# The split of wo moved from GpSimd between the stages to ScalarE and VectorE inside the last tile of the first stage

## The chip, the cores and the metric

The kernel runs on one core of a Trainium2 chip. The metric is the time of one execution on the device in microseconds, as the median of several runs; less is better.

## The reference

Two different blocks alternate, on the same x of 2048 rows and 640 columns, all in float32. In short:

```python
def A(x, wqkv, wo):                      # linear attention, 32 heads of 20
    q, k, v = split(x @ wqkv)            # each (head, row, 20)
    phi = lambda t: where(t > 0, t + 1, exp(t)) + 1e-6
    kv = einsum("hsd,hse->hde", phi(k), v)
    z = phi(k).sum(rows)
    o = (phi(q) @ kv) / (phi(q) . z + 1e-6)
    return merge_heads(o) @ wo

def B(x, w1, b1, w2, b2):                # 640 -> 1728 -> 640
    return relu(x @ w1 + b1) ** 2 @ w2 + b2

x = x + A(layernorm(x)); x = x + B(layernorm(x))
x = x + A(layernorm(x)); x = x + B(layernorm(x))   # the same weights again
```

## The kernel before

A pass over A and B is one layer; there are two, with the same code. Each float32 operand of a matmul is kept as a high part, which ScalarE rounds with a copy (`AF.Copy` to fp32r), and a low part, which is the rest and is made by a subtraction, as a rule on VectorE. A product is then three matmuls: high with low, low with high, high with high. `split(hi, lo, src)` does both parts; line 147 is its copy and line 148 its subtraction.

The order of the work on each engine is the order in which the code issues it, written out by hand. Nothing is reordered, so an instruction that waits holds up everything behind it on its engine.

**First stage** (loop at line 746): 16 tiles of 128 rows. For tile t, TensorE computes k and, for most tiles, q (`part`, line 508 through `mm3`, line 418). For the tiles listed in `LATE`, 14 and 15 among them, q is computed after the loop (`late_q`). phi is an exp on ScalarE (line 521) and two operations on VectorE (lines 528 and 529). `k_post` (line 724) splits phi(k) into `kh` and adds it into `acc` on GpSimd (line 731); `acc` is the sum of phi(k) from which z comes. kv is not formed from v: with xh the split normalised x, the stage sums G = xhᵀ·phi(k), in five row blocks of 128 (`g_part`, PSUM banks 3 to 7) for the first 512 columns of phi(k), and the last 128 columns transposed as GT (`gt_part`, one call for two tiles and half of the columns of x, added on VectorE at line 559).

During tiles 13 to 15, `load_vo` loads the v columns of wqkv, and wo in six chunks of 120 rows (the last has 40), into tiles called `uraw`.

**Between the stages** (lines 875 to 1176), in order of issue: two late q products; `ah`, the split of acc, and its column sums with a matrix of ones (line 913), copied to `zbc`; `b_den(0)`, which begins the denominators of tile 0; the last `g_part` of the five blocks, each with a ScalarE copy out of PSUM (line 926); the last two `gt_part`; the rest of `b_blocks(0)`; six `wo_high` copies on ScalarE (line 942, into tiles called `uo`) and six `wo_low` subtractions on GpSimd (line 946); five turns of GT on TensorE (line 387) and their copy Gs; kv for six blocks of heads (line 987), each masked on VectorE (line 992), copied and subtracted into `kvbd` (lines 993 and 997); then M = kv·wo for the six blocks (line 1011), three pairs of PSUM banks in turn. M goes through DRAM and comes back as `Mr`, while TensorE does further late q products; then the output products with M begin (line 439).

The masks of kv use banks 3, 4, 5, 6, 7, 2 in turn, and M the pairs (4,5), (2,3), (6,7): an M product waits for the masks that read its banks.

Tiles named x (xh, kh, ah, uo, pT, kvbd, Mr) share a ring of eight places; phi(k) of a tile, two of the uo and Gs share a ring of three.

**Second stage**: the block B in groups of 512 rows (lines 1229 and 1289), with A's output products for the next group inside it.

Of the kernel before, what the change touches and what calls it, by code (L numbers as in the profile page):

```python
# [8 lines left out]
F32 = mybir.dt.float32  # L9
R32 = mybir.dt.float32r  # L10
AF = mybir.ActivationFunctionType
ALU = mybir.AluOpType

P = 128
S, D, F = 2048, 640, 1728
H, DH = 32, 20
NT = S // P
# [13 lines left out]
NH = -(-D // HR)  # L31
# [53 lines left out]
def head_rows(c):  # L85
    return min(HR, D - HR * c)
# [3 lines left out]
def kernel(  # L90
# [11 lines left out]
    nc = tc.nc  # L102
# [13 lines left out]
    def bank(i, n=1):  # L116
        return PS[:, 512 * i : 512 * (i + n)]
# [23 lines left out]
    def ftile(name):  # L141
        return tmp.tile([P, D], F32, tag="f", name=name, bufs=F_BUFS)


    def split(hi, lo, src):

        nc.scalar.activation(hi, src, AF.Copy)
        nc.vector.tensor_tensor(out=lo, in0=src, in1=hi.bitcast(F32), op=ALU.subtract)  # L148
# [242 lines left out]
    def blocks_T(src):  # L391
        y = ftile("y")
        nc.vector.transpose(out=y, in_=src)  # L393
        return [y]

    def blocks_move(yz, js, vector=False):
        if len(yz) == 1:
            yz.append(ftile("z"))
        yv, zv = (a.rearrange("p (c j q) -> p c j q", c=DC, q=B32) for a in yz)
        for j in js:  # L400
            for i in range(P // B32):
                d, v = zv[j * B32 : (j + 1) * B32, :, i, :], yv[i * B32 : (i + 1) * B32, :, j, :]
                if vector:
                    nc.vector.tensor_copy(d, v)
                else:
                    nc.scalar.activation(d, v, AF.Copy)  # L406
# [7 lines left out]
    def mm3(ps, lh, ll, rh, rl, first, last):  # L414

        seq = [(lh, rl), (ll, rh), (lh, rh)]
        for i, (a, b) in enumerate(seq):
            nc.tensor.matmul(ps, a, b, start=first and i == 0, stop=last and i == 2)  # L418
# [54 lines left out]
    for layer in range(N_LAYERS):  # L473
        src = [rows(t, xf) for t in range(NT)] if layer == 0 else x2
        last_layer = layer == N_LAYERS - 1
        if layer == 0:
# [8 lines left out]
        ap = sg.enter_context(  # L485
            tc.tile_pool(name=f"a_{layer}", bufs=1, side="left", reuse_waits="tile")
        )
# [7 lines left out]
        acc = ap.tile([P, D], F32, name="acc", tag="acc", bufs=1)  # L495
# [4 lines left out]
        def xbank():  # L500
            xbanks.append(xbanks.pop(0))
            return bank(xbanks[-1])

        def part(t, a, b, ps=None):

            ps = (xbank() if ps is None else ps)[:, : b - a]
            for c in range(DC):
                mm3(
                    ps, xT[t][:, 0, c, :], xT[t][:, 1, c, :],
                    kq[c][:, 0, a:b], kq[c][:, 1, a:b], c == 0, c == DC - 1,  # L510
                )
            return ps
# [23 lines left out]
        def xtile(name, dtype=R32):  # L536
            return xp.tile([P, 2, D], dtype, tag="x", name=name, bufs=8)
# [12 lines left out]
        def gt_part(p, j, ps):  # L550

            ps, rs = ps[:, :HD], slice(j * HD, (j + 1) * HD)
            for t in (2 * p, 2 * p + 1):
                a, b = kh[t][:, :, DM:], xh[t][:, :, rs]
                mm3(ps, a[:, 0], a[:, 1], b[:, 0], b[:, 1], t % 2 == 0, t % 2 == 1)
            if p == 0:
                nc.vector.tensor_copy(GT_[:, rs], ps)
            else:
                nc.vector.tensor_tensor(out=GT_[:, rs], in0=ps, in1=GT_[:, rs], op=ALU.add)

        if layer == 0:
# [18 lines left out]
            for ps, a, b in runs:  # L580
                v = xt[0][:, a * P : b * P]
# [10 lines left out]
            for ps, a, b in runs:  # L592
                d = T4[0][:, 0, :, a * P : b * P]
                nc.vector.tensor_tensor(
                    out=d[:, 1], in0=ps[:, : (b - a) * P], in1=d[:, 0].bitcast(F32), op=ALU.subtract
# [16 lines left out]
            out=mask, in_=mask, compare_op=ALU.is_ge, fill=0.0, base=0,  # L612
# [3 lines left out]
            out=mask, in_=mask, compare_op=ALU.is_ge, fill=0.0, base=DH - 1,  # L616
# [3 lines left out]
        vo = {}  # L620
# [68 lines left out]
        def b_blocks(t):  # L689
            b_step(t, 3)  # L690
# [33 lines left out]
        def k_post(t, r, between=()):  # L724

            kh[t] = u = xtile("kh")
            nc.scalar.activation(u[:, 0], r, AF.Copy)
            if t == 0:
                nc.gpsimd.tensor_copy(acc, r)
            else:  # L730
                nc.gpsimd.tensor_tensor(out=acc, in0=acc, in1=r, op=ALU.add)  # L731
            for f in between:
                f()
            nc.vector.tensor_tensor(out=u[:, 1], in0=r, in1=u[:, 0].bitcast(F32), op=ALU.subtract)  # L734

        moved = {}

        def move(t, n=P // B32, vector=False):

            if t in yza:  # L740
                blocks_move(yza[t], range(moved.get(t, 0), n), vector)
                moved[t] = n

        late = LATE[layer]
        q_end = None
        for t in range(NT):
# [15 lines left out]
            if first:  # L762
# [35 lines left out]
                fq.rest()  # L798
                xh[t] = split_new(xt[t], "xh")
                k_post(t, fk.r)  # L800
                nc.sync.dma_start(pqd[0], fq.r)
                continue
# [12 lines left out]
            ps = ps_first if layer == 0 and t == 1 else part(t, 0, n0, bank(XB[0]))  # L815
            gs(0 if is_late or t == 1 and layer == 0 else 2)
            move(t + 1, vector=t in VMOVE)
            f.exp(0, ps)
            second = layer == 0 and t == 1
# [3 lines left out]
            elif not early and t + 2 < NT:  # L823
                a_apply(t + 2)
                yza[t + 2] = blocks_T(xt[t + 2])
            f.rest()
            gt = t % 2 == 0 and t > 0
            ps = part(t, n0, D if is_late else 1024, bank(XB[1]))
            if t + 1 in yza:
# [30 lines left out]
            else:  # L860
                ps = part(t, 1024, 2 * D, bank(XB[2]))
                gs(1)
            k_post(t, f.r, [lambda: a_stats(t + 3)])
            if gt and not is_late:
                gt_part(t // 2 - 1, 1, bank(XB[1]))
            gs(DC)
            if not is_late:

                def q_end(t=t, f=fq, ps=ps):
                    f.exp(1024 - D, ps)  # L870
                    f.rest()
                    nc.sync.dma_start(pqd[t], f.r)

            move(t + 2, AHEAD)
        if q_end:
            q_end()
# [6 lines left out]
        def late_q(n=1, rest=True):  # L883

            for _ in range(n):
                if not late_parts:
                    return
                t, j = late_parts.pop(0)
                if j == 0:
                    late_phi[t] = Phi(ftile("rl"))  # L890
                late_phi[t].exp(j * HD, part(t, D + j * HD, D + (j + 1) * HD))
                late_todo.append((t, j))
                if rest:
                    late_rest()
# [3 lines left out]
        def late_rest(n=9):  # L898
            for _ in range(min(n, len(late_todo))):
                t, j = late_todo.pop(0)  # L900
                late_phi[t].rest()
                if j == 1:
                    nc.sync.dma_start(pqd[t], late_phi.pop(t).r)

        late_q(1)
        ah = xtile("ah")
        split(ah[:, 0], ah[:, 1], acc)
        late_q(1)
        zbc = tmp.tile([P, R_], F32, tag="z", name="zbc", bufs=1)
        psz = [xbank()[:, :HD] for _ in range(2)]  # L910
# [5 lines left out]
        for j in range(JB):  # L916
            p, k = slice(j * B32, (j + 1) * B32), j % 2
            v = psz[j // 2][p, k * R_ : (k + 1) * R_]
# [5 lines left out]
        for i in range(DC):  # L924
            g_part(NT - 1, i)
            nc.scalar.activation(G[:, i], bank(GB[i]), AF.Copy)
        for j in range(2):
            gt_part(NT // 2 - 1, j, xbank())
        b_blocks(0)

        wo_hi = {}

        def wo_high(i):
            n = head_rows(2 * i + 1)
            if i < 2:
                v = xtile("uo")
                wo_hi[2 * i], wo_hi[2 * i + 1] = v[:, 0], v[:, 1]
            else:
                wo_hi[4], wo_hi[5] = (ap.tile([P, D], F32, tag="r", name="uo", bufs=3).bitcast(R32) for _ in range(2))
            for c in (2 * i, 2 * i + 1):  # L940
                n = head_rows(c)
                nc.scalar.activation(wo_hi[c][:n], vo["o", c][:n].bitcast(F32), AF.Copy)

        def wo_low(c):
            n, v = head_rows(c), vo["o", c]
            nc.gpsimd.tensor_tensor(
                out=v[:n], in0=v[:n].bitcast(F32), in1=wo_hi[c][:n].bitcast(F32), op=ALU.subtract
            )

        for i in range(3):  # L950
            wo_high(i)
        for c in range(NH):
            wo_low(c)

        psT = bank(1, 2)
        transpose5(psT, GT_)
# [768 lines left out]
```

## Time and profile before

| | |
|---|---|
| time, median of 3 runs | 1345.42 us (1345.09 to 1345.6) |
| the profiled execution's own time | 1347.59 us |
| its span, first to last instruction | 1345.8 us |
| mean granted TensorE clock | 0.999 |
| TensorE busy | 1334.4 us (99%) |
| VectorE busy | 903.6 us (67%) |
| ScalarE busy | 708.9 us (53%) |
| GpSimd busy | 144.8 us (11%) |

All durations of single instructions come from the profiled execution. PE is TensorE's matmuls and PEld its weight loads, DVE is VectorE, ACT is ScalarE, POOL is GpSimd, SP is the engine that issues most transfers. In a timeline a line has the start and the length in microseconds, engine, line of the code, operation, output and inputs, and in brackets how long the engine had stood idle and who released it. Instructions of one kind that follow each other are merged into one line with their count, and the length is then that of the whole series.

### The profile page before, as it was taken

What the parts mean: (1) busy time and instruction counts of PE and PEld (TensorE: products, weight loads), DVE (VectorE), ACT (ScalarE), POOL (GpSimd) and SP (SyncE); (2) the same over time, 40 slices, a digit from 0 to 9 for tenths busy, and PEclk for the clock granted to TensorE, in tenths of its full rate; (3) what the DMA queues carried; (4) which work ended last, traced back from release to release, by engine and by line L of the source; (5) the groups of instructions that cost most, each with busy time, mean ns of one, the idle gap of its engine ahead of it and who ended that gap; (6) DMA issues with size and microseconds to landing.
All of it is one profiled execution on the core that took longest, in us unless ns stands there. A gap on an engine that the chain in (4) does not pass through costs nothing.

```text
span 1345.8 us, 18849 instructions
## 1 busy us (share of the span) xinstructions
PE 1334.4 (99%) x6770; PEld 1156.1 (86%) x6770; DVE 903.6 (67%) x1613; ACT 708.9 (53%) x1636; POOL 144.8 (11%) x183
## 2 busy tenths in 40 slices
PE   9999999999999999999999999999999999999998
PEld 7888999988888888888888899898888888888887
DVE  8988879877766756543367678688677567665323
ACT  5888854634545426424547686455435535454131
POOL 2222221100000000000012232400000000000000
PEclk9999999999999999999999999999999999999999
DMA  6788835775557476487521115077447565564644
GB/s 205 254 294 318 274 98 160 241 273 174 194 200 234 134 258 184 158 308 290 203 98 53 46 40 153 24 242 264 153 161 270 162 202 190 213 213 142 250 165 158
DMA packets 100687, 257.53 MB, mean 191 GB/s; under 512 B 12802, under 2 KB 37762, under 8 KB 99922
## 3 DMA queue, kind: packets, MB, share of 16 engines
q1 hardware_dynamic: 99370, 253.68, 55.8%
q10 hardware_dynamic: 1224, 2.65, 0.7%
q8 instruction: 53, 0.87, 0.3%
q14 instruction: 40, 0.33, 0.1%
HBM read 197.60 MB, written 60.13 MB: 191 GB/s over the span
## 4 chain that ended last, share of the span: by engine, by line
PE 96%; DVE 3%; DMA 1%; ACT 0%; SPq 0%; issue 0%; POOL 0%; DVEq 0%; ACTq 0%
PE PS L418 36%; PE PS L1289 28%; PE PS L1229 28%; PE PS L439 3%; PE PS L1011 1%; DMA st<-in_A_wqkv_dram 1%; DVE kvbd L997 0%; DVE pT L148 0%; DVE e L528 0%; DVE r L529 0%; DVE pqt L671 0%; DVE bn L373 0%; PE PS L387 0%; SPq L226 0%; ACT kq L204 0%
## 5 line engine op out<-in xcount | busy, mean ns | idle before, releaser
L1229 PE MATMUL PS<-xTb,u 128*128 128x512 f32 x1400 | 332.8, 390 | 0.0
L406 ACT ACTIVATE z<-y 32x160 f32<-32x160 f32 x880 | 294.0, 334 | 61.0 <-DVE y L393 51.1
L1229 PEld LDWEIGHTS PS<-xTb,u 128*128 128x128 f32 x1400 | 262.3, 188 | 53.7
L418 PE MATMUL PS<-kq,xT 128*128 128x320 f32 (+2 forms) x1575 | 282.3, 334 | 0.0
L1289 PE MATMUL PS<-u,h 128*128 128x512 f32 x1120 | 279.6, 390 | 0.0
L418 PEld LDWEIGHTS PS<-kq,xT 128*128 128x128 f32 x1575 | 250.3, 188 | 25.2 <-DVE xT L148 0.2
L1247 ACT ACTIVATE hr<-PS,b1sb 128x512 f32<-128x512 f32 x104 | 71.5, 687 | 348.9 <-PE PS L1229 347.3
L1289 PEld LDWEIGHTS PS<-u,h 128*128 128x128 f32 x1120 | 208.0, 188 | 39.6
L1251 DVE TENSOR_TENSOR hr<-hr 128x512 f32<-128x512 f32 x104 | 71.3, 685 | 148.7 <-ACT h L1248 148.7
L418 PE MATMUL PS<-kh,xh 128*128 128x512 f32 x480 | 124.1, 392 | 0.9 <-DVE kh L734 0.8
L377 POOL TENSOR_SCALAR rs<-mv 128x1 f32<-128x1 f32 x63 | 28.8, 457 | 823.6 <-DVE mv L375 823.6
L521 ACT ACTIVATE e<-PS 128x320 f32<-128x320 f32 (+4 forms) x128 | 53.3, 435 | 100.4 <-PE PS L418 92.3
L418 PEld LDWEIGHTS PS<-kh,xh 128*128 128x128 f32 x480 | 87.2, 188 | 16.0 <-DVE kh L734 1.2
L528 DVE TENSOR_SCALAR e<-e 128x320 f32<-128x320 f32 (+4 forms) x128 | 42.9, 335 | 64.5 <-ACT e L521 64.2
L1289 PE MATMUL PS<-h,u 128*128 128x512 f32 x280 | 79.1, 391 | 0.0
L1252 DVE TENSOR_TENSOR h<-hr,h 128x512 fp32r<-128x512 f32 x104 | 72.0, 693 | 7.5
L731 POOL TENSOR_TENSOR acc<-acc,r 128x640 f32<-128x640 f32 x30 | 53.9, 1796 | 197.4 <-DVE r L529 197.4
L1248 ACT ACTIVATE h<-hr 128x512 fp32r<-128x512 f32 x104 | 65.8, 633 | 3.7 <-DVE uT L148 0.5
L1289 PEld LDWEIGHTS PS<-h,u 128*128 128x128 f32 x280 | 52.0, 188 | 10.5 <-DVE h L1265 0.4
L1497 DVE TENSOR_TENSOR xr<-PS,xr 128x320 f32<-128x320 f32 x48 | 23.5, 489 | 51.8 <-PE PS L418 50.2
L1229 PE MATMUL PS<-xTb,uw 128*128 128x512 f32 x240 | 57.0, 389 | 0.0
L529 DVE SCALAR_TENSOR_TENSOR r<-PS,e 128x512 f32<-128x512 f32 (+2 forms) x104 | 51.1, 492 | 5.8 <-ACT e L521 2.3
(142 smaller groups left out, 1599.7 us busy)
## 6 DMA issues: line engine op xcount, KB each, us to landing
u<-kept_w SPq DMA_DIRECT2D x184, 640.0 KB, 4.7
x<-x SPq DMA_DIRECT2D x48, 320.0 KB, 4.8
kept_w<-uprep SPq DMA_DIRECT2D x23, 640.0 KB, 5.5
pqt<-pq SPq DMA_DIRECT2D x128, 80.0 KB, 4.5
x<-xr SPq DMA_DIRECT2D x32, 320.0 KB, 2.3
st<-in_B_w_dram SPq DMA_DIRECT2D x22, 320.0 KB, 3.4
pq<-r SPq DMA_DIRECT2D x20, 320.0 KB, 2.4
kept_kq<-kq SPq DMA_DIRECT2D x10, 640.0 KB, 5.6
```

Of the source, the lines that this page charges most:

```text
L406: nc.scalar.activation(d, v, AF.Copy)
L418: nc.tensor.matmul(ps, a, b, start=first and i == 0, stop=last and i == 2)
L521: nc.scalar.activation(self.e[:, a:b], ps, AF.Exp)
L528: nc.vector.tensor_scalar(e, e, 1.0, PHI_EPS, op0=ALU.min, op1=ALU.add)
L529: nc.vector.scalar_tensor_tensor(out=self.r[:, a:b], in0=ps, scalar=0.0, in1=e, op0=ALU.max, op1=ALU.add)
L731: nc.gpsimd.tensor_tensor(out=acc, in0=acc, in1=r, op=ALU.add)
L1229: nc.tensor.matmul(ps, a[:, d, :], bb[:, d, :], start=n == 0, stop=n == len(order) - 1)
L1247: nc.scalar.activation(r, ps, AF.Relu, bias=b1sb[:, c : c + 1])
L1248: nc.scalar.activation(h[:, 0], r, AF.Square)
L1251: nc.vector.tensor_tensor(out=r, in0=r, in1=r, op=ALU.mult)
L1252: nc.vector.tensor_tensor(out=h[:, 1], in0=r, in1=h[:, 0].bitcast(F32), op=ALU.subtract)
L1289: nc.tensor.matmul(ps, l, r, start=first and k == 0, stop=last and k == len(a) - 1)
```

## The change

1. `wo_high` and `wo_low` are defined ahead of the loop over tiles. `wo_low` runs on VectorE.
2. In tile 15, after phi of the first half of k and ahead of the second half's product, the first four chunks of wo are split: two copies, two subtractions, two copies, two subtractions.
3. The last two chunks are split right after `ah`, ahead of the second late q product.
4. The last two `gt_part` are issued after the third of the five last `g_part`, in place of after the fifth.
5. In layer 0, tiles 1 and 2, the addition of phi(k) into `acc` is done by VectorE, behind the subtraction that makes the low part of `kh`, in place of by GpSimd ahead of it.

```diff
@@ k_post
             if t == 0:
                 nc.gpsimd.tensor_copy(acc, r)
-            else:
+            elif not (layer == 0 and t in (1, 2)):
                 nc.gpsimd.tensor_tensor(out=acc, in0=acc, in1=r, op=ALU.add)
             for f in between:
                 f()
             nc.vector.tensor_tensor(out=u[:, 1], in0=r, in1=u[:, 0].bitcast(F32), op=ALU.subtract)
+            if layer == 0 and t in (1, 2):
+                nc.vector.tensor_tensor(out=acc, in0=acc, in1=r, op=ALU.add)
@@ ahead of the loop over tiles: wo_high as before, and
+        def wo_low(c):
+            n, v = head_rows(c), vo["o", c]
+            nc.vector.tensor_tensor(
+                out=v[:n], in0=v[:n].bitcast(F32), in1=wo_hi[c][:n].bitcast(F32), op=ALU.subtract
+            )
@@ in the loop
             f.rest()
+            if t == NT - 1:
+                wo_high(0)
+                wo_low(0)
+                wo_low(1)
+                wo_high(1)
+                wo_low(2)
+                wo_low(3)
             gt = t % 2 == 0 and t > 0
             ps = part(t, n0, D if is_late else 1024, bank(XB[1]))
@@ after the loop
         split(ah[:, 0], ah[:, 1], acc)
+        wo_high(2)
+        wo_low(4)
+        wo_low(5)
         late_q(1)
@@
         for i in range(DC):
             g_part(NT - 1, i)
             nc.scalar.activation(G[:, i], bank(GB[i]), AF.Copy)
-        for j in range(2):
-            gt_part(NT // 2 - 1, j, xbank())
+            if i == 2:
+                for j in range(2):
+                    gt_part(NT // 2 - 1, j, xbank())
         b_blocks(0)
-
-        wo_hi = {}
-
-        def wo_high(i):
...
-        def wo_low(c):
-            n, v = head_rows(c), vo["o", c]
-            nc.gpsimd.tensor_tensor(
-                out=v[:n], in0=v[:n].bitcast(F32), in1=wo_hi[c][:n].bitcast(F32), op=ALU.subtract
-            )
-
-        for i in range(3):
-            wo_high(i)
-        for c in range(NH):
-            wo_low(c)
```

More of the change, by code (lines that the diff above doesn't have):

```diff
@@ L742, in move, with wo_high @@
                 moved[t] = n
+        wo_hi = {}
+        def wo_high(i):
+            n = head_rows(2 * i + 1)
+            if i < 2:
+                v = xtile("uo")
+                wo_hi[2 * i], wo_hi[2 * i + 1] = v[:, 0], v[:, 1]
+            else:
+                wo_hi[4], wo_hi[5] = (ap.tile([P, D], F32, tag="r", name="uo", bufs=3).bitcast(R32) for _ in range(2))
+            for c in (2 * i, 2 * i + 1):
+                n = head_rows(c)
+                nc.scalar.activation(wo_hi[c][:n], vo["o", c][:n].bitcast(F32), AF.Copy)
+        def wo_low(c):
[3 more added lines that the diff above has]
+            )
         late = LATE[layer]
@@ L926 @@
             nc.scalar.activation(G[:, i], bank(GB[i]), AF.Copy)
-        for j in range(2):
-            gt_part(NT // 2 - 1, j, xbank())
+            if i == 2:
+                for j in range(2):
+                    gt_part(NT // 2 - 1, j, xbank())
         b_blocks(0)
-        wo_hi = {}
-        def wo_high(i):
[L934 to L942, printed above, removed]
-        def wo_low(c):
-            n, v = head_rows(c), vo["o", c]
-            nc.gpsimd.tensor_tensor(
-                out=v[:n], in0=v[:n].bitcast(F32), in1=wo_hi[c][:n].bitcast(F32), op=ALU.subtract
-            )
-        for i in range(3):
-            wo_high(i)
-        for c in range(NH):
-            wo_low(c)
         psT = bank(1, 2)
```

## The prediction

> **What bounds the kernel now.** I read the page first: its first part (busy time), then the chain that ended last.
>
> ```profile
> span 1345.8 us, 18849 instructions
> PE 1334.4 (99%) x6770; PEld 1156.1 (86%) x6770; DVE 903.6 (67%) x1613; ACT 708.9 (53%) x1636; POOL 144.8 (11%) x183
> ...
> PE 96%; DVE 3%; DMA 1%; ACT 0%; SPq 0%; issue 0%; POOL 0%; DVEq 0%; ACTq 0%
> ```
>
> TensorE holds 96% of the chain and the 11.4 us in which it is idle are all that an edit of the other engines can win, beside time in which its clock is lowered. The change adds and removes no matmul. So the next view is the list of TensorE's own waits, cut to the lines that the change can reach:
>
> ```profile
> PE PS L1011 <- DVE kvr L992: 3.7, 4, 1.4
> ...
> PE PS L418 <- DVE kh L734: 0.8, 1, 0.8
> PE PS L387 <- DVE GT L559: 0.7, 2, 0.4
> ```
>
> These 5.2 us are two waits for VectorE in each layer between the stages (the products M = kv·wo at L1011, the turns of GT at L387) and one in the first tiles (L418). Whoever made VectorE late is seen in the timeline of the first layer's stretch between the stages:
>
> ```profile
> 198.26 10.28 POOL L946 TENSOR_TENSOR uraw<-uraw,uo 120x640 fp32r<-120x640 f32 x6 [9.87 <-ACT uo L942]
> ...
> 198.52 0.38 PE L387 MATMUL PS<-ident,GT 128*128 128x128 f32 x2
> 198.72 0.49 DVE L559 TENSOR_TENSOR GT<-PS,GT 128x320 f32<-128x320 f32 x1 [0.39 <-PE PS L418]
> ...
> 199.27 0.55 PE L387 MATMUL PS<-ident,GT 128*128 128x128 f32 x3 [0.37 <-DVE GT L559]
> ...
> 199.65 5.34 PE L987 MATMUL PS<-G,uraw 128*120 128x120 f32 x50
> ...
> 203.69 1.90 DVE L148 TENSOR_TENSOR pT<-z,pT 128x640 fp32r<-128x640 f32 x1 [0.80 <-ACT pT L147]
> ...
> 206.52 0.41 PE L1011 MATMUL PS<-uo,kvbd 120*120 120x320 f32 x1
> ...
> 207.25 1.43 DVE L997 TENSOR_TENSOR kvbd<-kvr,kvbd 120x120 fp32r<-120x120 f32 x1
> ...
> 207.38 0.70 PE L1011 MATMUL PS<-uo,kvbd 120*120 120x320 f32 x3 [0.45 <-DVE kvr L992]
> ...
> 208.80 0.27 DVE L997 TENSOR_TENSOR kvbd<-kvr,kvbd 120x120 fp32r<-120x120 f32 x1
> ...
> 209.77 0.82 PE L1011 MATMUL PS<-uo,kvbd 120*120 120x320 f32 x4 [1.40 <-DVE kvr L992]
> ...
> 214.57 10.62 PE L418 MATMUL PS<-kq,xT 128*128 128x320 f32 x71
> ...
> 220.47 0.82 DVE L148 TENSOR_TENSOR pT<-z,pT 128x640 fp32r<-128x640 f32 x1
> ```
>
> GpSimd splits wo from 198.26 to 208.54. While it does, VectorE's operations with two inputs in SBUF are long: the split of pT takes 1.90 us against 0.82 at 220.47, a small subtraction at L997 takes 1.43 against 0.27 at 208.80, just after GpSimd's last. So the masks of kv are late, and the second M product, which takes over the PSUM bank of the last mask, starts at 209.77. The same stretch of the second layer by windows (span, then busy time and count of PE, PEld, DVE, ACT, POOL, then the granted clock):
>
> ```profile
> 871.00:874.20 3.20, 1.35 (x7) 0.86 (x7) 3.20 (x9) 1.00 (x4) 1.99 (x2) 1.00 0.00 0
> 874.20:880.50 6.30, 6.28 (x30) 5.70 (x31) 6.07 (x11) 3.51 (x7) 0.00 (x0) 0.73 0.60 161
> ```
>
> TensorE idles 1.85 us here, as in the first layer (0.45 and 1.40), but in the second its granted clock is 0.73 right afterwards. The chain gives the price of that, the same thirty matmuls in both layers:
>
> ```profile
> 209.77 4.95 PE PS L1011 x30
> ...
> 874.22 6.49 PE PS L1011 x30
> ```
>
> **Between the stages, per layer.** GpSimd's six subtractions go (10.28 us, cover: none is needed, they only run elsewhere), ScalarE's six wo copies leave the place ahead of Gs, and the two GT products are issued before the last two columns of G. TensorE then does, without waiting: five turns, from 198.52, in 0.76 us (198.52 to 199.65 less the idle 0.37; GT's sums now run under the six matmuls of the last two columns); kv, as before, 6.87 us (199.65 to 206.52); M, 36 matmuls at 0.160 us (30 in the 4.80 us from 209.77 to 214.57), 5.76 us. End: 198.52 + 0.76 + 6.87 + 5.76 = 211.91, against 214.57, which is 2.66 us earlier. From below, only the idle time goes: 0.37 + 0.45 + 1.40 = 2.2. From above, M at TensorE's pitch of the late products (71 in 10.62, 0.150): 3.0. I take 2.66, since its pitch is that of the same instructions with ScalarE's copies behind them. VectorE's part is ready: at 198.1 (below) with GT, then 0.18 to 0.84 us each for den, its inverse, the product and the transpose, 0.82 for pT, and masks at 0.27 as soon as kv is there. It must have the last mask by the second M product, near 207.4; it needs 0.3 us after kv ends at 206.2.
>
> What follows moves along: ScalarE's copies of M start 2.5 us earlier, the transfers through DRAM with them, and the late products fill TensorE's time until M is back. The next to be late would be bank 7, which the third late product needs (30 matmuls, 4.5 us, after M's end, so near 216.4) and which ScalarE empties in these copies:
>
> ```profile
> 216.01 2.85 ACT L1034 ACTIVATE Mr<-PS 32x640 f32<-32x640 f32 x4
> ```
>
> Now they end at 218.86, with TensorE there at 219.1; moved by 2.5 to 2.9 us they end about when TensorE comes, and cost nothing to 0.3 us, which lies in the bounds.
>
> **Inside the last tile, per layer.** The moved work, and the places that take it:
>
> ```profile
> 182.72 0.44 ACT L521 ACTIVATE e<-PS 128x320 f32<-128x320 f32 x1 [4.50 <-PE PS L418]
> ...
> 183.55 0.49 DVE L529 SCALAR_TENSOR_TENSOR r<-PS,e 128x320 f32<-128x320 f32 x1
> ...
> 184.92 0.44 ACT L521 ACTIVATE e<-PS 128x320 f32<-128x320 f32 x1 [1.76 <-PE PS L418]
> ...
> 185.39 0.33 DVE L528 TENSOR_SCALAR e<-e 128x320 f32<-128x320 f32 x1 [1.35 <-ACT e L521]
> ...
> 187.04 2.04 DVE L734 TENSOR_TENSOR kh<-r,kh 128x640 fp32r<-128x640 f32 x1
> ...
> 191.00 0.33 DVE L528 TENSOR_SCALAR e<-e 128x320 f32<-128x320 f32 x1 [1.93 <-ACT e L521]
> ...
> 193.20 0.33 DVE L528 TENSOR_SCALAR e<-e 128x320 f32<-128x320 f32 x1 [0.61 <-ACT e L521]
> ...
> 197.46 3.86 ACT L942 ACTIVATE uo<-uraw 120x640 fp32r<-120x640 f32 x6
> ```
>
> ScalarE: four copies at 0.63 (3.86 us for six) from 183.16 end at 185.7; the second exp, behind them, comes at 185.7 in place of 184.92, 0.8 us late. VectorE: four subtractions at 0.77 to 0.82 (as L148 at 220.47) from 184.04 end at 187.1 to 187.3, so the second half of phi(k) starts 1.7 to 1.9 us late, and with it xh, kh and GpSimd's sum. The queue behind has room of 1.93 us, the wait at 191.00, before ah, which TensorE needs at 192.65 for the column sums: cost 0, at most 0.3. kh and xh of tile 15 are needed only after those. The last two pieces stand behind ah's split: two copies delay the next exp by 0.1; two subtractions of 0.8 less the wait of 0.61 at 193.20 put VectorE 1.0 us back, so den's sum ends near 197.4 and GT's two sums (0.49 each) near 198.3, before the turns at 198.52. If they are later, the turns wait as now: that is the 0.37 again.
>
> No transfer is added. The uo tiles now come out of the ring of eight x tiles ahead of xh and kh of tile 15, so two of the three Mr tiles fall on their places; a read of M's rows into these has to follow the products that read uo, which it does anyway, since it reads what those products wrote to DRAM: 0. Rows of wo must have landed by 183.2 to 185.1 instead of 197.5; their issue on SP does not move.
>
> **First tiles of layer 0.** GpSimd's sums for tiles 1 and 2 go; VectorE gets one 0.77 us addition each, behind kh's low half.
>
> ```profile
> 30.96 1.56 POOL L731 TENSOR_TENSOR acc<-acc,r 128x640 f32<-128x640 f32 x1 [2.11 <-DVE r L529]
> 31.02 1.72 DVE L528 TENSOR_SCALAR e<-e 128x384 f32<-128x384 f32 x1
> ...
> 31.48 3.56 PE L418 MATMUL PS<-kq,xT 128*128 128x512 f32 x15
> ...
> 35.03 0.77 DVE L734 TENSOR_TENSOR kh<-r,kh 128x640 fp32r<-128x640 f32 x1
> ...
> 35.85 1.66 PE L418 MATMUL PS<-kh,xh 128*128 128x512 f32 x6 [0.81 <-DVE kh L734]
> ...
> 42.73 0.35 DVE L528 TENSOR_SCALAR e<-e 128x384 f32<-128x384 f32 x1
> ```
>
> The 1.72 is the same shape that takes 0.35 at 42.73, before GpSimd starts. Without the sum, VectorE is 1.37 us earlier: kh ends at 34.43, before TensorE is free at 35.04, so the whole 0.81 goes. The addition then ends at 35.2, still 0.6 us ahead of today's queue. Tile 2 pays 0.77 and is freed of a like delay: 0. Bounds 0 and 0.81; I take 0.81, as the chain runs through this row.
>
> **The sum.** 0.81 + 2 x 2.66 = 6.1 us. The profiled execution took 1347.59 us around its span of 1345.8, and would lose these and the 1.54 of lowered clock: 7.7, to 1339.9. The median is 2.17 us below that execution, more than the lowered clock alone, so I take the timed runs to be without it: 1345.42 - 6.1 = 1339.3 us.
>
> The Trainium skill (TensorE: Matmul & The Clock Gate, "What's actually happening") says that the clock falls to half for windows of 3.4 us that run free of the kernel. The trace agrees as far as it goes: one stretch of lowered clock that cost 1.54 us, in one layer of two alike. By that rule a timed run may have none, one or two, and the sum would be 6.1, 7.7 or 9.2.
>
> **Rivals.** A: the timed runs have one lowered stretch, and it goes too: 6.1 + 1.54, so 1337.8. For it, the idle 1.85 us ahead of it; against it, that layer 0 has the same idle time and no drop.
>
> B: half is given back, at ah, at the turns (0.37) or at bank 7 (0.3 to 1): all are within 0.3 us of binding. At 1.4 us a layer: 1342.1.
>
> C: the change does not free VectorE, since its long rows have another cause than GpSimd. Then only GT's 0.37 a layer goes: 1344.7. Against it: the rows shorten exactly when GpSimd stops. The Trainium skill (SBUF — State Buffer, "Who interferes with whom") says the two share a port pair under an exclusive lock; by that rule C is excluded, and the rows agree.
>
> D, slower: ScalarE is in order, and waits in tile 15 for rows of wo, with phi(k) of the tile behind it.
>
> ```profile
> 171.13 3.42 SPq L632 DMA_DIRECT2D uraw<-wod  x4
> ...
> DMA to landing us min/median/max: 4.4/6.9/8.0
> ```
>
> The last is issued by 174.5 and, at 8.0 us, landed by 182.5; it is needed at 185.1. It costs us for us past 185.3, in both layers, and makes the kernel slower by 2.7 us only when it is 4.4 us later than that, 15 us after issue: 1348.1 and up. Against it, the longest landing seen.
>
> **How the numbers follow.** A change under 0.2% (2.7 us) can hardly be told from none. Forecast 1339.3: 0.60; A 0.16; B 0.12; C 0.06; D 0.06. Faster holds the first three, 0.88; same 0.06; slower 0.06. The range goes from A with M at the higher pitch (0.34 a layer, 0.7) and 0.4 more for part of a second stretch, 1336.7, to B and another 0.5 at its places, 1342.6.
>
> **What would show it.** No GpSimd row between 193 and 207; L148 and L997 there at 0.82 and 0.28; turns without a wait; M products from one to the next with no wait over 0.3 us, starting near 205.3 (206.15 less the 0.81 of the first tiles); the first tiles' wait at L418 gone; the granted clock 1.00 in both layers. Wrong: a wait at the column sums (L913) over 0.3 us, exp at L521 in tile 15 later than 186, a wait of the late products for L1034, or VectorE falling behind in tiles 3 to 6.

## The result

| | before | changed |
|---|---|---|
| time, median of 6 runs each | 1346.16 us (1345.09 to 1349.5) | 1339.04 us (1338.52 to 1339.38) |
| ratio, 95% interval | | 0.9944 (0.9931 to 0.9957) |
| the profiled execution's own time | 1347.59 us | 1339.24 us |
| its span | 1345.8 us | 1337.5 us |

The changed kernel is 0.56% faster. The six runs before are the three known at the forecast and three more, which took 1346.72, 1347.08 and 1349.5 us. The page of the changed kernel, the parts that answer to those of before:

```profile
span 1337.5 us, 18840 instructions
PE 1332.0 (100%) x6770; PEld 1154.7 (86%) x6770; DVE 902.0 (67%) x1627; ACT 708.3 (53%) x1636; POOL 121.9 (9%) x169
...
PE 97%; DVE 1%; ACT 1%; issue 0%; ACTq 0%; POOL 0%; DVEq 0%; POOLq 0%
```

TensorE's own waits, the whole list of the changed kernel:

```profile
PE PS L567 <- POOL ident masks.py:199: 1.4, 1, 1.4
PE PS L418 <- ACT Mr L1043: 0.3, 1, 0.3
```

The three waits for VectorE (M, GT, kh) are gone. A new one of 0.3 us stands in their place: in layer 1 a late product waits for ScalarE's copies of M. The timeline between the stages of layer 0 (the lines of the code have moved: the column sums are now L945, kv L996, its mask L1001, its low part L1006, M L1020):

```profile
190.84 0.85 PE L945 MATMUL PS<-ah,ones 128*128 128x320 f32 x4
...
196.75 0.71 PE L387 MATMUL PS<-ident,GT 128*128 128x128 f32 x5
196.86 0.83 DVE L671 TENSOR_TENSOR pqt<-pqt,den 128x640 f32<-128x640 f32 x1
197.29 5.34 PE L996 MATMUL PS<-G,uraw 128*120 128x120 f32 x50
...
199.37 0.82 DVE L148 TENSOR_TENSOR pT<-z,pT 128x640 fp32r<-128x640 f32 x1 [0.80 <-ACT pT L147]
...
200.82 0.28 DVE L1006 TENSOR_TENSOR kvbd<-kvr,kvbd 120x120 fp32r<-120x120 f32 x1 [0.24 <-ACT kvbd L1002]
...
204.27 0.19 DVE L1001 TENSOR_TENSOR kvr<-PS,mask 40x40 f32<-40x40 f32 x1
...
205.14 0.75 PE L1020 MATMUL PS<-uo,kvbd 120*120 120x320 f32 x4
...
209.86 11.48 PE L418 MATMUL PS<-kq,xT 128*128 128x320 f32 x75
...
214.48 6.60 PEld L418 LDWEIGHTS PS<-kq,xT 128*128 128x128 f32 x45 [0.33 <-ACT Mr L1043]
```

VectorE's rows are at 0.82 and 0.28, the last mask ends 0.7 us before the second M product (204.46 and 205.14), and the late products start at 209.86 in place of 214.57. The third of them then waits for bank 7 (here the weight load, PEld, waits 0.33 us). The granted clock is 1.00 in the stretch between the stages of both layers.

The 8.3 us of span, by how far the same row has moved from one profile to the other: 0.83 us is gained before the first changed instruction, in the load of the first weights, and belongs to no edit: the profiles of the experiments pass the same row between 0.9 us earlier and 0.3 us later than the kernel before, and the first of experiment 4, whose code is the same up to there, passes it 0.73 us earlier. The first tiles bring 0.97 (the wait of 35.85 now reads 34.05). Layer 0 brings 2.90 up to the late products (column sums moved by 1.81, late products by 4.71) and loses 0.28 at bank 7. Layer 1 brings 4.45, of which 1.54 is the stretch of lowered clock, and loses 0.56 at bank 7. The column sums of layer 0 before, for the first of these differences:

```profile
192.65 0.85 PE L913 MATMUL PS<-ah,ones 128*128 128x320 f32 x4
```

### The profile page after: what moved, and what is told of

It reads as the page before. It is cut to its first block, busy times and chain, and to the rows that moved or that the text cites. A ratio compares the mean times of both kernels' runs of the same rounds, so it can differ in the third digit from the quotient of the medians.

```text
span 1337.5 us, 18840 instructions
## 1 busy us (share of the span) xinstructions
PE 1332.0 (100%) x6770; PEld 1154.7 (86%) x6770; DVE 902.0 (67%) x1627; ACT 708.3 (53%) x1636; POOL 121.9 (9%) x169
## 4 chain that ended last, share of the span: by engine, by line
PE 97%; DVE 1%; ACT 1%; issue 0%; ACTq 0%; POOL 0%; DVEq 0%; POOLq 0%
PE PS L418 36%; PE PS L1298 28%; PE PS L1238 28%; PE PS L439 3%; PE PS L996 1%; PE PS L794 0%; ACT Mr L1043 0%; PE PS L567 0%; PE PS L1020 0%; PE PS L387 0%; DVE kq L210 0%; DVE r L529 0%; DVE e L528 0%; DVE den L662 0%; DVE pr L655 0%
## 5 line engine op out<-in xcount | busy, mean ns | idle before, releaser
L418 PE MATMUL PS<-kq,xT 128*128 128x320 f32 (+2 forms) x1575 | 282.7, 334 | 0.4 <-ACT Mr L1043 0.3
L418 PEld LDWEIGHTS PS<-kq,xT 128*128 128x128 f32 x1575 | 250.2, 188 | 26.1 <-ACT Mr L1043 0.9
L418 PE MATMUL PS<-kh,xh 128*128 128x512 f32 x480 | 124.4, 392 | 0.0
L418 PEld LDWEIGHTS PS<-kh,xh 128*128 128x128 f32 x480 | 87.1, 188 | 14.8 <-DVE xT L148 0.2
L528 DVE TENSOR_SCALAR e<-e 128x320 f32<-128x320 f32 (+4 forms) x128 | 41.4, 323 | 57.6 <-ACT e L521 57.1
L731 POOL TENSOR_TENSOR acc<-acc,r 128x640 f32<-128x640 f32 x28 | 50.7, 1811 | 191.3 <-DVE r L529 191.3
```

The costliest lines, as they stand in the source:

```text
L528: nc.vector.tensor_scalar(e, e, 1.0, PHI_EPS, op0=ALU.min, op1=ALU.add)
```

## The experiments

The kernel before does not keep one time. In its 44 runs beside the experiments, time and mean granted clock go together: 1344.94 to 1345.29 us at 1.000 (4 runs), 1346.48 to 1347.35 at 0.999 (7), 1347.92 to 1348.64 at 0.997 (17), 1350.93 to 1351.12 at 0.995 (9), and the other seven in between. Steps of about 1.5 us fit the price of one lowered stretch in the profile of before (6.49 less 4.95 = 1.54). So differences below are taken from runs at the same clock, or from waits in the profile.

**1. GpSimd silent, the place kept.** Only the engine of the six subtractions is changed, in `wo_low` between the stages:

```diff
-            nc.gpsimd.tensor_tensor(
+            nc.vector.tensor_tensor(
```

> The six subtractions of wo go from GpSimd to VectorE, at their old place between the stages; nothing else is changed. Theory (GpSimd's reads hold VectorE's two-input operations): with GpSimd silent, L671 falls from 1.73 to 0.83, pT's L148 from 1.90 to 0.82, L997 from 1.43 to 0.28, which saves VectorE 4.3 us and costs it 4.6 (six at 0.77); the masks end about 0.9 us earlier, since the long L997 stood last; 1 to 2 us faster in all, a half-clock stretch of the kernel before set aside. Rival (VectorE's rows are long for another cause): they stay long, VectorE is 4.6 us later in each layer, some 8 us slower.

Measured: 1343.82 us (1343.43 to 1344.42), ratio 0.9964 (0.9951 to 0.9977), with the granted clock at 1.000 in all five runs. Against before at clock 1.000 that is 1.3 us faster, as the theory had it. In the timeline of this kernel:

```profile
199.42 0.83 DVE L671 TENSOR_TENSOR pqt<-pqt,den 128x640 f32<-128x640 f32 x1
...
201.05 4.45 DVE L946 TENSOR_TENSOR uraw<-uraw,uo 120x640 fp32r<-120x640 f32 x6
205.42 0.81 DVE L148 TENSOR_TENSOR pT<-z,pT 128x640 fp32r<-128x640 f32 x1
...
206.87 1.21 PE L1011 MATMUL PS<-uo,kvbd 120*120 120x320 f32 x4 [0.59 <-ACT kvbd L993]
```

The long rows fall to 0.83 and 0.81 as soon as GpSimd does no work there, which goes against rival C. But VectorE's own 4.45 us take nearly all of it back, and the M products still wait 0.8 us a layer in place of 1.85. The engine alone is worth about a fifth of the change; the place has to change too.

**2. The place changed, GpSimd kept.** The changed kernel with `nc.gpsimd` in `wo_low`.

> The whole change, but the six subtractions of wo stay on GpSimd, inside tile 15 and after ah. Theory: the stretch between the stages is as short as in the changed kernel, but in tile 15 GpSimd's sum of phi(k) stands behind four subtractions of about 1.6 to 1.9 us, ends near 191 in place of 188.1, ah comes 2 to 3 us late, and TensorE waits that long ahead of the column sums in each layer: 4 to 6 us slower than the changed kernel, 2 to 4 faster than the kernel before. Rival (only the place matters, not the engine): within 0.5 us of the changed kernel.

Measured: 1345.4 us (1344.44 to 1346.07), ratio 0.9980 (0.9971 to 0.9989), 6.4 us above the changed kernel and 2.8 below the kernel before of its own chip (1348.22). Its timeline in tile 15:

```profile
182.35 6.86 POOL L762 TENSOR_TENSOR uraw<-uraw,uo 120x640 fp32r<-120x640 f32 x4 [4.25 <-ACT uo L758]
...
189.16 2.15 POOL L731 TENSOR_TENSOR acc<-acc,r 128x640 f32<-128x640 f32 x1
...
193.00 0.85 PE L945 MATMUL PS<-ah,ones 128*128 128x320 f32 x4 [1.81 <-DVE ah L148]
```

The sum of phi(k) stands behind the four subtractions, ah is late, and TensorE waits 1.81 us in each layer. The rest of the 6.4 is clock. By windows (the granted clock is the third number from the end; the second window follows the wait of layer 0, the third that of layer 1):

```profile
188.00:196.00 8.00, 6.19 (x32) 5.48 (x31) 6.99 (x9) 3.87 (x8) 6.49 (x4) 0.87 0.01 3
196.00:204.00 8.00, 8.00 (x56) 7.36 (x55) 5.76 (x11) 3.92 (x7) 0.00 (x0) 0.92 0.28 79
...
858.00:866.00 8.00, 7.74 (x34) 6.66 (x35) 5.72 (x12) 3.90 (x9) 3.17 (x2) 0.79 0.29 86
```

What is missing from 1.00 comes to 3.4 us in this execution, which took 1346.07. The expected 4 to 6 us had left the clock out. The rival (only the place matters) is out.

**3. GpSimd's work put back, without its data.** Unused subtractions on GpSimd between the stages of the changed kernel.

```diff
         b_blocks(0)
+        for _ in range(6):
+            nc.gpsimd.tensor_tensor(out=acc[:, :DM], in0=G[:, DC - 1], in1=G[:, DC - 1], op=ALU.subtract)
```

> The changed kernel with six subtractions on GpSimd between the stages that nothing uses (128x512, read from the last column block of G, written over the dead acc), about 1.4 us each, 8 us in all from the end of G's last copy. Theory: VectorE's operations with two inputs in SBUF are long again (L671, pT's L148, L1006 up to 1.4), the masks come 2 to 3 us late, and the M products wait 0.5 to 1.5 us in each layer: 1.5 to 4 us slower than the changed kernel. Rival (it was the wo data or ScalarE's copies that held the stretch up, not GpSimd's activity): within 0.3 us of the changed kernel.

Measured: 1339.04 us (1338.53 to 1339.62), beside 1338.92 for the changed kernel on the same chip: nothing, as the rival said. The trace shows why: VectorE's rows did get longer (L148 1.08, the low part of kv up to 1.00), but GpSimd took 1.18 us for one, not 1.4, and ended at 204.84. The last mask came at 204.90 in place of 204.27, and that was still ahead of the second M product (205.26 in place of 205.14; this profile starts 0.13 later). So VectorE had room for this delay, and the run by itself does not tell the rival from a dose too small. Eight longer ones decide it:

```diff
+        Gf = G.rearrange("p c n -> p (c n)")[:, DC * DM - D :]
+        for _ in range(8):
+            nc.gpsimd.tensor_tensor(out=acc, in0=Gf, in1=Gf, op=ALU.subtract)
```

> The changed kernel with eight unused subtractions on GpSimd between the stages, as in the run before with six, but over 640 columns (both inputs the last 640 columns of G), about 1.6 us each, some 13 us from the end of G's last copy, so that GpSimd is busy past the last mask of kv, as it was in the kernel before. Theory: pT's L148 and each of the first four L1006 take 1.0 to 1.7 us, the last mask comes near 207 in place of 204.5, the second M product waits about 2 us in each layer, and stretches of lowered clock come back: 4 to 8 us slower than the changed kernel. Rival (the six shorter subtractions cost nothing because GpSimd's reads do not reach TensorE at all): within 0.3 us.

Measured: 1341.13 us (1341.02 to 1341.24). Its timeline:

```profile
197.65 11.84 POOL L965 TENSOR_TENSOR acc<-G 128x640 f32<-128x640 f32 x8 [9.51 <-ACT G L958]
...
199.41 1.50 DVE L148 TENSOR_TENSOR pT<-z,pT 128x640 fp32r<-128x640 f32 x1 [0.80 <-ACT pT L147]
...
203.62 1.22 DVE L1009 TENSOR_TENSOR kvbd<-kvr,kvbd 120x120 fp32r<-120x120 f32 x1
...
206.42 0.82 PE L1023 MATMUL PS<-uo,kvbd 120*120 120x320 f32 x4 [1.09 <-DVE kvr L1004]
```

The wait of the second M product is back, 1.1 us in each layer, and the time is 2.2 us above the changed kernel, as the two waits give. The expected 4 to 8 was too much twice over: the wait is 1.1 and not 2, and no stretch of lowered clock came with it. The rival is out. These reads bring back 1.1 of the 1.85 us that the kernel before waits in each layer; the wo split itself took 1.71 us for one subtraction against 1.48 here, and what the rest of its wait hangs on was not separated. The same with writes in place of reads:

```diff
+        nc.gpsimd.tensor_tensor(out=acc, in0=Gf, in1=Gf, op=ALU.subtract)
+        for _ in range(16):
+            nc.gpsimd.memset(acc, 0.0)
```

> The same with one subtraction and then sixteen memsets of 128x640 on GpSimd, which write and read nothing. Theory (it is GpSimd's reads that hold VectorE's second input): L148 and L1006 are long at most during the first 1.6 us and 0.82 and 0.28 after it, and the time is within 0.5 us of the changed kernel. Rival (any work of GpSimd in SBUF holds VectorE): as with the reads, some us slower.

Measured: 1338.87 us (1338.74 to 1338.95), the changed kernel's time.

```profile
198.83 7.54 POOL L966 MEMSET acc<- 128x640 f32 x11
199.29 0.82 DVE L148 TENSOR_TENSOR pT<-z,pT 128x640 fp32r<-128x640 f32 x1 [0.80 <-ACT pT L147]
...
206.55 0.55 DVE L668 TENSOR_SCALAR den<-den 128x32 f32<-128x32 f32 x1
```

GpSimd is busy all the while, and VectorE's row is 0.82. It is GpSimd's reading of SBUF that holds VectorE's operations with two inputs there. The Trainium skill (SBUF — State Buffer, "Who interferes with whom") says just this, for GpSimd instructions that read and not for those that only write; both halves agree with these two runs. The last line above is another case: a TENSOR_SCALAR, with one input from SBUF, took 0.55 us beside a memset, against 0.17 elsewhere. In these traces this operation is held by GpSimd's writes too; nothing waited for it here.

**4. The GT order, alone and left out.** Part 4 on the kernel before, and the changed kernel without it.

> Only part 4 of the change: the last two GT products stand after the third of the last five columns of G; GpSimd still splits wo between the stages. Theory (GpSimd's split holds VectorE): the 0.37 us wait of the turns goes in each layer, but ScalarE now copies the last two columns of G about 1.9 us later, so the wo copies behind them and GpSimd's six subtractions start and end about 2 us later (near 210.5 in place of 208.5), VectorE's short subtractions wait for them as long, and the second M product starts 0 to 1.5 us later than 209.77. In all 0 to +2 us against the kernel before. Rival (each part of the change brings its own share): 0.7 us faster, 0.37 in each layer.

Measured: 1350.49 us (1349.76 to 1353.82), ratio 1.0016 (1.0005 to 1.0027): slower, as the theory had it. The medians are 2.3 us apart (the kernel before has 1348.22 on this chip); at a clock of 0.997 it is 1349.76 to 1349.96 against 1347.92 to 1348.64, some 1.6 us. From the list of TensorE's waits and the timeline:

```profile
PE PS L1012 <- ACT kvbd L994: 5.0, 2, 2.5
...
PE PS L1012 <- DVE kvr L993: 1.4, 2, 0.7
```

```profile
199.34 9.72 POOL L947 TENSOR_TENSOR uraw<-uraw,uo 120x640 fp32r<-120x640 f32 x6 [11.66 <-ACT uo L943]
```

The turns no longer wait, but G's last copies stand ahead of the wo copies, GpSimd starts later, and the M products wait 3.2 us a layer in place of 1.85, with clocks of 0.994 to 0.997 in the runs.

> The changed kernel without part 4: the two GT products stand after the fifth last column of G again. Theory: TensorE waits 0.37 us ahead of the turns in each layer, and VectorE's chain behind GT's sums starts 0.8 us later, which is covered until the masks: 0.7 us slower than the changed kernel. Rival (the later start of VectorE's chain reaches the M products): 1.5 us or more slower.

Measured: 1340.19 us (1339.73 to 1340.45), 1.3 above the changed kernel's 1338.9. The wait ahead of the turns is back in each layer, and there is none at the M products:

```profile
196.65 0.38 PE L387 MATMUL PS<-ident,GT 128*128 128x128 f32 x2
...
197.39 0.55 PE L387 MATMUL PS<-ident,GT 128*128 128x128 f32 x3 [0.36 <-DVE GT L559]
...
197.77 5.34 PE L995 MATMUL PS<-G,uraw 128*120 128x120 f32 x50
```

From the first turn to kv TensorE takes 1.12 us, against 0.54 in the changed kernel (196.75 to 197.29). A series broken by a wait of 0.36 us costs 0.58 more, not 0.36. Some of it comes back at bank 7, and the span of the profile is 0.7 us longer. So the sign of this edit hangs on wo being gone from behind it.

**5. The first tiles alone.** Part 5 on the kernel before.

> Only part 5: VectorE adds phi(k) for tiles 1 and 2 of layer 0. Theory: L528 at 31.0 falls from 1.72 to 0.36, the wait of TensorE at L418 for kh (0.81) goes, all later rows come 0.8 to 1.0 us earlier, the M wait of both layers stays: 0.8 to 1.0 us faster. Rival (VectorE, nearly full in these tiles, pays the two additions later on): 0.

Measured: 1347.5 us (1345.71 to 1350.2), ratio 0.9998 (0.9987 to 1.0009), which by itself decides nothing, since the lowered clock is in most of the runs. At equal clock it does: 1347.1 to 1347.63 at 0.997, against 1347.92 to 1348.64 before. The wait at L418 is gone in the profile, and L528 takes 0.36 in place of 1.72:

```profile
30.37 0.36 DVE L528 TENSOR_SCALAR e<-e 128x384 f32<-128x384 f32 x1
...
34.22 1.52 PE L418 MATMUL PS<-kh,xh 128*128 128x512 f32 x6
```

That is about 0.9 us, as the theory had it.

**6. The room in tile 15.** All six chunks split inside tile 15.

> The changed kernel with the last two chunks of wo also split inside tile 15, behind the first four, in place of behind ah. Theory (VectorE's room ahead of ah, of which 0.42 us is left in the changed kernel): two more subtractions of 0.77 put VectorE 1.5 us back, ah's low half comes 1.1 us late, and TensorE waits 1.1 us at the column sums in each layer: 2.2 us slower than the changed kernel. Rival (the wait of 0.42 is no limit since ScalarE or TensorE have room elsewhere): no change.

Measured: 1341.03 us (1340.74 to 1341.17), 2.1 above the changed kernel.

```profile
191.76 0.85 PE L945 MATMUL PS<-ah,ones 128*128 128x320 f32 x4 [0.90 <-DVE ah L148]
```

Two more subtractions use up the room, and TensorE waits 0.90 us in each layer, where 1.1 was expected.

**7. Bank 7.** The third late product in bank 2, the fourth in bank 7.

```diff
-        xbanks = [7]
+        xbanks = [2]
         late_q(1, False)
...
-        xbanks = [2, 3, 0, 1]
+        xbanks = [7]
         late_q(1, False)
         m_split(2)
+        xbanks = [3, 0, 1, 2]
         late_q(1, False)
```

> The changed kernel with the third late product in bank 2 and the fourth in bank 7 (bank 3 for the fifth as before), since in the changed kernel the third waits 0.2 to 0.5 us for ScalarE to empty bank 7 in each layer. Theory: both waits go, no other comes: 0.7 us faster than the changed kernel. Rival (M itself, back from DRAM, is late next): the first product with M waits instead, no gain.

> The changed kernel as it is, timed on the same chip as the other three, for comparison: 1339 us on a chip where the kernel before takes 1345.4 to 1346.2, ratio 0.994 to 0.996, no stretch of lowered clock.

Measured: 1338.45 us (1338.17 to 1340.03) against 1338.92 (1338.68 to 1339.12) for the changed kernel, whose ratio of 0.9935 was a little below what was expected because the kernel before stood at 1347.92 and not at 1345.4 to 1346.2. The profiled execution of the new order is the 1340.03; its start took 1.1 us longer than that of the changed kernel. The late products now run without a gap, and M read back from DRAM is the next to be late, once in layer 1, in part as the rival said:

```profile
210.96 11.16 PE L418 MATMUL PS<-kq,xT 128*128 128x320 f32 x75
```

```profile
PE PS L439 <- DVE uM L1079: 0.3, 1, 0.3
```

It may be the better version, by 0.5 us of median, but the ranges of the two overlap, so this is not shown.

## Why the prediction was right

The forecast was 1339.3 us; the runs gave 1339.04. In the profiles the parts of the sum bring 0.97 + 2.62 + 2.35 = 5.94 us, where it had 6.13.

- **Between the stages** (2.66 us a layer, bounds 2.2 and 3.0): measured 2.90 and 2.91 up to the late products, near the upper bound. Kv took 6.87 us as in the sum and M 5.70 in place of 5.76, which is 0.158 us a matmul and not the 0.150 of that bound. What was too small was the gain at the turns: the sum took off only the idle 0.37 and left them 0.76 us, and unbroken they took 0.54. Experiment 3 shows the cause that was named, GpSimd's reads.
- **Bank 7** (0 to 0.3): named as the next to be late, and it was, at 0.28 and 0.56; a wait of the late products for these copies was also listed as a sign of being wrong, and that sign came. In layer 1 the bound was passed, for a reason that the prediction did not have: ScalarE also issues the transfers of M, and one issue ahead of the copies took 0.83 us in place of 0.32 (0.67 in the other profile of the changed kernel, beside experiment 7). Why that issue was long is open. With bank 7 taken off, a layer brings 2.62 and 2.35, together 0.35 less than the sum had.
- **First tiles** (0.81, bounds 0 and 0.81): 0.97 in the profile, above the bound. The wait was 0.81; the six matmuls behind it also went from 1.66 to 1.52 us. The row that held VectorE up there (L528) is a TENSOR_SCALAR with one input, so the prediction's "operations with two inputs" is too narrow for this part.
- **Inside tile 15** (second half of phi 1.7 to 1.9 late, cost 0): of the room of 1.93 us, 0.42 is left, so 1.5 was used, and the column sums wait no longer than before (0.21 at the weight load in both). Experiment 6 confirms where the room ends.

The rows behind the last point, after:

```profile
181.25 2.61 ACT L758 ACTIVATE uo<-uraw 120x640 fp32r<-120x640 f32 x4
...
182.15 3.02 DVE L762 TENSOR_TENSOR uraw<-uraw,uo 120x640 fp32r<-120x640 f32 x4
...
189.20 0.33 DVE L528 TENSOR_SCALAR e<-e 128x320 f32<-128x320 f32 x1 [0.42 <-ACT e L521]
...
190.84 0.59 PEld L945 LDWEIGHTS PS<-ah,ones 128*128 128x128 f32 x4 [0.21 <-DVE ah L148]
```

The rows of the long issue in layer 1:

```profile
868.98 0.32 ACTq L1028 DMA_DIRECT2D md<-Mc  x1
...
870.22 0.83 ACTq L1028 DMA_DIRECT2D md<-Mc  x1
...
876.51 6.61 PEld L418 LDWEIGHTS PS<-kq,xT 128*128 128x128 f32 x45 [0.56 <-ACT Mr L1043]
```

- **The clock.** The choice to read the first three runs of before as free of lowered clock fits these: 1345.09 to 1345.6 is close to the level of the runs at 1.000. It does not fit most others. From runs at full clock the gain is 6.3 us (1345.2 to 1338.9), next to the forecast's 6.1. The medians of the result are 7.1 apart and those of the runs beside experiment 7 9.0 (1347.92 and 1338.92), near the 9.2 that the prediction worked out for two lowered stretches. So rival A had the clock right for 40 of the 44 runs beside the experiments, which stand below 1.000; its time of 1337.8 did not come, since it starts from three runs that were not of that kind.
- Of rival B only bank 7 came: ah and the turns gave nothing back. Rivals C and D did not come: experiments 1 and 3 exclude C, and no wait for rows of wo shows in tile 15, where ScalarE's four copies follow each other at 0.65 (2.61 us for four).

The mechanism was right, and the number was also lucky twice: larger gains at the turns and in the first tiles nearly cancel the loss at bank 7, and the three runs that the forecast starts from were at full clock.

## What to carry to other kernels

When an operation on VectorE with two inputs in SBUF, or a TENSOR_SCALAR, is much longer in one stretch than elsewhere, look for a GpSimd instruction beside it; if the chain runs through VectorE there, move GpSimd's work to where VectorE waits, and count that room by the idle time ahead of the next operation that the critical engine needs. Edits around one wait are not additive: the GT order alone cost time and beside the other edits saved it. A wait of TensorE of 1.8 us cost some 1.5 us more by the clock here when its place was caught, and how often it did shows in the granted clock of many runs, not in a single profile.

## What the runs showed of the hardware

- Lowered clock went with short idle times. Of the 13 profiles, four have stretches of lowered clock, six in all, and each stands at or behind a place where TensorE had idled 1.8 us or more within 5 us: the kernel before and experiment 5 (1.85 us) in layer 1 only, experiment 2 (1.81, in one wait) and the first of 4 (3.2) in both layers. Over the 8 us in which each lies most fully the clock reads 0.79, so 1.7 us of clock is missing; in the kernel before the thirty matmuls there took 1.54 us longer. Kernels with 1.1 us of idle time or less in such a place (experiments 1, 3, 6) show none, and their runs stand at 0.999 to 1.000, those of the four others at 0.994 to 0.999 in nearly all cases. Where between 1.1 and 1.8 us the limit lies, and which layer is caught, was not tried. The slowest runs of the kernel before, 5.8 us above its fastest, would need more lowered stretches than the two of any trace; where those lie is open.
- GpSimd's own duration depends on VectorE too: the same subtraction over 640 columns took 1.25 us where VectorE ran a transpose with one input beside it, and 1.48 on average in the series of eight, with VectorE's two-input operations beside it. In the split of wo of the kernel before, with other operands, it took 1.71.
- A TENSOR_SCALAR on VectorE is held as well: 128x384 took 1.72 us beside GpSimd's sum and 0.36 without it, and 128x32 took 0.55 and 0.61 beside memsets (experiment 3), which only write, against 0.17.
